# Issuing a kernel's stores from ScalarE's queue in place of SyncE's

## The chip, the core and the metric

The kernel runs on one NeuronCore of a Trainium2 chip. Five engines take their instructions from queues of their own, in order: TensorE (PE; its weight loads are listed as PEld), VectorE (DVE), ScalarE (ACT), GpSimd (POOL) and SyncE (SP). SP computes nothing; in this kernel it issues every transfer (DMA) between the chip's memory and the on-chip buffers. The metric is the device time of one execution in microseconds (us), the median of several runs.

## The reference

Two independent layers are computed over 2048 positions and 576 channels, and their outputs stand side by side in the result (columns 0 to 575 and 576 to 1151).

```python
# A: a state-space layer (S4D) as a long convolution
P = exp((A * dt[:, None])[:, :, None] * pos[None, None, :])        # A, C complex, 576 x 128
K = 2.0 * einsum("dn,dnl->dl", C, P).real                          # one filter per channel
y = irfft(rfft(u_t, 2 * L) * rfft(K, 2 * L)[None], 2 * L)[:, :, :L]
a = y.transpose(0, 2, 1) + u * D_skip

# B: linear attention, 32 heads of 18, with a learned feature map
q, k, v = split_heads(x @ wqkv)
pq, pk = q @ w_phi, k @ w_phi                                      # per head
phi_q = concat([softmax(pq), softmax(-pq)]); phi_k = the same of pk
kv, z = phi_k^T v, sum of phi_k over positions
o = (phi_q kv) / (phi_q z + 1e-6)
b = merge_heads(o) @ wo
out = concat([a, b], axis=-1)
```

All inputs and the output are 32-bit floats.

## The kernel before, in words

**Layer B.** The positions are cut into 16 tiles of 128. `key_tile` loads a tile of x, splits it into a rounded part and a remainder (`x9`, kept in memory as `xd` for later: the split x, stored at L546), multiplies it with the folded key and value weights in three passes per weight, takes the two softmaxes (`softmax`: exponentials on ACT, sums on POOL and DVE) and adds up `kv`. `query_tile` loads `xd` again (L552), makes the query features, transposes them (`fT`), multiplies with `kv`, divides, transposes and splits the result (`x9` again), multiplies with `wo` and copies the product to a tile `ot`, which L739 stores to the output.

**Layer A.** The filters' values come from `phases` (integer angles, on POOL), `waves` (absolute value, sine and cosine on ACT, L909 to L917, which need another function table than the exponentials do, so table loads stand between), and `group` (magnitudes by a product with `sel` and an exponential on ACT, L933 and L940; their products with the waves, `cs` and `E`, on DVE and POOL; and a TensorE product `ps<-E,cs`). The convolution is done by a Fourier transform in two stages, whose first and second stages meet in memory: `u_first` transforms the input u and stores 32 pieces of `ud` (L769, one pair for each of 16 steps); `k_first` does it for the filters and stores 16 pieces of `kd` (L983). These are the two first transforms. `product` loads them (`ub`, `kb`) with its factors (`ff`, L1024), multiplies the spectra and stores the way back to `zd` (L1097, 32 pieces); it starts only when all pieces of `ud` have landed. `last` loads `zd` (L1107), does the final stage and stores rows of the output from tiles `yo` (L1122, 32 pieces). Tiles `zi`, `zo`, `ot` are filled from TensorE's results by copies of ACT and DVE, in shares that the order table fixes.

**What sets the order.** `body` first lists about 2900 operations with their engine, then `Plan.run` gives them out in the order of a table in the file, `ORDER` (L277 on). A number in it is an operation, "*" takes its second engine, "/n" gives the buffer and "+n" adds filler products. Each engine gets its own operations in this one order, so a store's place in the table is also its place in the queue that issues it. The framework adds the semaphores: an issue waits for the writers of its tile, and for transfers that it has to follow. The name in quotes in an `op(...)` call ("sp") is used by the list and its costs; the engine that issues is the one whose `dma_start` is called.

Some places of the table matter below. Store 2446 (L1097, `product` 1) stands behind the DVE copy 2444 and ahead of the ACT operations 2301, 2299, 2302 (L916, L916, L917). Stores 1237, 1238, 1317, 1318, 1198 and 1197 (L769) follow ACT's copies of their tiles. Store 2803 (L1122, `last` 1) stands ahead of ACT's copy 2330 and a table load. Stores 2900 and 2901 (L1122, `last` 15) stand between ACT's two copies 1107 and 1109 of `fT`. The last two operations of the table are ACT's copy 853 of `ot` and its store 854.

Of the kernel before, what the change touches and what calls it, by code (L numbers as in the profile page):

```python
# [266 lines left out]
def c_dma(nbytes, run=4096):  # L267
    return nbytes / run * (0.35 + 0.0029 * run)
# [158 lines left out]
def body(tc, nc, i, out, ctx):  # L427
    pl = Plan()
    pe, dve, act, pool, sp = nc.tensor, nc.vector, nc.scalar, nc.gpsimd, nc.sync
# [14 lines left out]
    B, op = pl.buf, pl.op  # L444
# [236 lines left out]
    def query_tile(t):  # L681
        pl.at("query", t)
        ps = gemm_halves(load_again(t), wqo, (have_q[0:3], have_q[2:5]), 0)
        pl.step("q1")
        e = softmax([(ps[c], slice(16 * c, 16 * c + 16), lambda c=c: ps[c].t.rearrange("p (h f) -> p h f", f=DH)) for c in range(2)], True)
        pl.step("q3")
        fT = []
        rows = lambda j: 18 * GRP[j // 2]

        def turn(j0, n):  # L690
            tp, m, f4 = B("ps", [126, 4, 128]), rows(j0), B("fT", [126, 4, 128])
            fT.append(f4)

            def f():
                for j in range(j0, j0 + n):
                    g, sign = divmod(j, 2)
                    pe.transpose(tp.t[0:m, j - j0, :], e.t[:, sign, 7 * g:7 * g + GRP[g], :].rearrange("p h f -> p (h f)"), ident.t)  # L697
            op("pe", 110 * n, f, r=[e, ident], w=[tp], with_=[f4], busy=0.5)
            copy("any", lambda: f4.t[0:m, 0:n, :], lambda: tp.t[0:m, 0:n], [tp], [f4], 128 * n)
        for j0, n in ((0, 4), (4, 4), (8, 2)):  # L700
            turn(j0, n)
        pl.step("q4")
        o = B("o", [128, H, DH])

        def divide(g0, g1, h0, n):
            pn, den = B("ps", [128, 21, 19]), B("small", [128, 21])

            def f():
                for g in range(g0, g1):
                    hs, m = slice(7 * g, 7 * g + GRP[g]), rows(2 * g)  # L710
                    for sign in range(2):
                        j = 2 * g + sign
                        mm(pn.t[:, hs.start - h0:hs.stop - h0], fT[j // 4].t[0:m, j % 4, :], kvb.t[0:m, sign, 0:GRP[g], g, :], sign == 0, sign == 1)
            op("pe", 448 * (g1 - g0), f, r=[*fT[g0 // 2:(2 * g1 - 1) // 4 + 1], kvb], w=[pn], busy=0.4)
            op("dve", 80 + 6.7 * n, lambda: dve.reciprocal(den.t[:, :n], pn.t[:, :n, 18]), r=[pn], w=[den])
            tt("dve", lambda: o.t[:, h0:h0 + n], lambda: pn.t[:, :n, 0:18], lambda: den.t[:, :n, None].to_broadcast([128, n, DH]),
               ALU.mult, [pn, den], [o], 18 * n)
        divide(0, 3, 0, 21)
        divide(3, 5, 21, 11)
        pl.step("q5")  # L720
        tp, tq = B("ps", [128, 4, 128]), B("ps", [128, 128])
        of = lambda c: o.t.rearrange("p h f -> p (h f)")[:, c:c + 128]

        def f():
            for k in range(4):
                pe.transpose(tp.t[:, k], of(128 * k), ident.t)  # L726
            pe.transpose(tq.t, of(448), ident.t)
        op("pe", 550, f, r=[o, ident], w=[tp, tq], busy=0.5)
        o9 = B("x9", [128, 9, 128], F32R)
        copy("act", lambda: o9.t[:, 0:4], lambda: tp.t, [tp], [o9], 512)  # L730
        tt("dve", lambda: o9.t[:, 5:9], lambda: tp.t, lambda: o9.t[:, 0:4].bitcast(F32), ALU.subtract, [tp, o9], [o9], 512)
        copy("act", lambda: o9.t[64:128, 4], lambda: tq.t[64:128], [tq], [o9], 260)
        tt("dve", lambda: o9.t[0:64, 4], lambda: tq.t[64:128], lambda: o9.t[64:128, 4].bitcast(F32), ALU.subtract, [tq, o9], [o9], 245)
        pl.step("q6")
        po = gemm_halves(o9, wqo, (have_o[0:2], have_o[1:3]), D)
        ot = B("ot", [128, D])
        for c, cs in enumerate(halves):
            copy("any", lambda c=c, cs=cs: ot.t[:, cs], lambda c=c: po[c].t, [po[c]], [ot], 288)
        op("sp", c_dma(128 * 2304, 2304), lambda: sp.dma_start(out[t * 128:t * 128 + 128, 576:1152], ot.t), r=[ot])  # L739

    for t in range(NT):
        query_tile(t)
# [9 lines left out]
    def u_first(k):  # L752
        us, uq, o = B("ub", [128, 2, HD]), B("kb", [128, 2, HD]), B("zi", [128, 4, HD])
        op("sp", c_dma(128 * 2304), lambda: sp.dma_start(us.t.rearrange("p a b -> p (a b)"), i["u"][:, D * k:D * k + D]), w=[us])
        for z, alu in enumerate((ALU.add, ALU.subtract)):
            tt(FLEX, lambda z=z: uq.t[:, z], lambda: us.t[:, 0], lambda: us.t[:, 1], alu, [us], [uq], HD)
        ps = [B("ps", [128, HD]) for _ in range(4)]
        pl.step("u1")

        def f():  # L760
            for z in range(2):
                for m in range(4):
                    rows = slice(32 * m, 32 * m + 32)
                    mm(ps[m].t[64 * z:64 * z + 64], w1.t[rows, 512 + 64 * z:][:, 0:64], uq.t[rows, z])
        op("pe", 520, f, r=[w1, uq], w=ps, with_=[o], mode=(32, 64))
        for m in range(4):
            copy("any", lambda m=m: o.t[:, m], lambda m=m: ps[m].t, [ps[m]], [o], HD)
        for z in range(2):
            op("sp", c_dma(64 * 4608), lambda z=z: sp.dma_start(  # L769
                ud.t[:, 32 * z + 2 * k:32 * z + 2 * k + 2].rearrange("p b d -> p (b d)"), o.t[64 * z:64 * z + 64].rearrange("p m d -> p (m d)")), r=[o], w=[ud])  # L770

    for k in range(16):
# [196 lines left out]
    def k_first(qt, ks):  # L969
        def one(j):  # L970
            o, ps = B("zi", [128, 8, 4, DQ]), [B("ps", [128, 8, DQ]) for _ in range(4)]

            def f():
                for s in range(2):
                    for m in range(4):
                        b0, rows = 8 * (j % 2), slice(32 * m, 32 * m + 32)
                        mm(ps[m].t.rearrange("p b d -> p (b d)"), w1.t[rows, 256 * (j // 2) + 128 * s:][:, 0:128],
                           ks[j // 2].t[rows, s, b0:b0 + 8, :].rearrange("p b d -> p (b d)"), s == 0, s == 1)
            op("pe", 970, f, r=[w1, ks[j // 2]], w=ps, with_=[o], mode=(32, 128))
            for m in range(4):  # L980
                copy("any", lambda m=m: o.t[:, :, m], lambda m=m: ps[m].t, [ps[m]], [o], HD)
            c0, d = qt % 2 * 4 * DQ, kd[qt // 2]
            op("sp", 1.3 * c_dma(128 * 4608, 576), lambda: sp.dma_start(  # L983
                d.t.rearrange("q (r b) d -> (q r) b d", r=2)[:, 8 * j:8 * j + 8, c0:c0 + 4 * DQ],
                o.t.rearrange("p b f d -> p b (f d)")), r=[o], w=[d])
        for j in range(4):
            one(j)
# [8 lines left out]
    par = [None] * NB  # L996
# [21 lines left out]
    def product(p, half):  # L1018
# [75 lines left out]
            copy("any", lambda c=c, j=j, par=par: zo[par].t[:, j], lambda c=c: pz[c].t, [pz[c]], [zo[par]], HD)  # L1094

        for par in range(2):
            op("sp", c_dma(128 * 2304, 1152), lambda par=par: sp.dma_start(four(zd[half], par), zo[par].t), r=[zo[par]], w=[zd[half]])  # L1097

    for half in range(2):
        for p in range(8):  # L1100
# [3 lines left out]
    def last(i0, half):  # L1104
        pl.at("last", 8 * half + i0 // 2)
        yo, zi = B("yo", [128, 2, HD]), B("zi", [128, 2, 2, HD])
        op("sp", c_dma(128 * 4608, 2304), lambda: sp.dma_start(  # L1107
            zi.t, zd[half].t.rearrange("q (r z b) d -> (q r) z b d", r=2, z=2)[:, :, i0:i0 + 2]), r=[zd[half]], w=[zi])
        ps = [B("ps", [128, HD]) for _ in range(2)]
        pl.step("l1")  # L1110

        def f():
            for z in range(2):
                for n in range(2):
                    mm(ps[z].t[64 * n:64 * n + 64], w3.t[:, 64 * z:64 * z + 64], zi.t[:, z, n], True, True, True)
        op("pe", 970, f, r=[zi, w3], w=ps, with_=[yo], mode=(128, 64))
        copy("any", lambda: yo.t[:, 1], lambda: ps[1].t, [ps[1]], [yo], HD)
        for z, alu in enumerate((ALU.add, ALU.subtract)):
            tt("dve", lambda z=z: yo.t[:, z], lambda: ps[0].t, lambda: yo.t[:, 1], alu, [ps[0], yo], [yo], HD)
        for n in range(2):  # L1120
            st = out.ap[0][0]
            op("sp", c_dma(64 * 2304, 1152), lambda n=n: sp.dma_start(bass.AP(  # L1122
                tensor=out.tensor, offset=out.offset + (i0 + n) * st + HD * half, ap=[[32 * st, 64], [(31 - 2 * (i0 + n)) * st, 2], [1, HD]]),
                yo.t[64 * n:64 * n + 64]), r=[yo])

# [25 lines left out]
```

## Time and profile before

| | |
|---|---|
| median of 3 runs | 540.35 us (539.47 to 544.67) |
| profiled execution | 542.0 us, of which the span from first to last instruction 540.2 us |
| PE, DVE, ACT, POOL busy | 519.9, 449.5, 413.8, 331.0 us |
| moved by DMA | 116.41 MB, mean 215 GB/s, all the kernel's own on one queue (q1) |

How to read it: a row of the timeline gives start and length in us, engine, line, operation, tile written <- tiles read, shape and count, and in brackets the idle time before it with what ended it. In the chain of waits a row is start, length and what. SPq and ACTq are the sequencers, which issue and wait and are not counted as busy. In a row of waits stand the total, the number of times and the longest. In a row of one source line come the count and the shortest, median and longest duration in ns, then the first and the last start. In the rows by windows the columns are the stretch, its length, and PE, PEld, DVE, ACT and POOL busy with their counts, then granted clock, share of the DMA engines and GB/s. Lines such as L447 (a product) and L452 (a copy) are helpers that many callers share, so a row is known by its tiles. Matmuls are pipelined, and their ends are modelled.

### The profile page before, as it was taken

Reading aid. Unit: us, or ns where it says so; the run is one execution under the profiler, and the core shown is the slowest. Engines: PE = TensorE matmul, PEld = TensorE weight load, DVE = VectorE, ACT = ScalarE, POOL = GpSimd, SP = SyncE. Lnnn points to the kernel's source line nnn. Section 1 sums busy time; section 2 is a strip of 40 time slices with the busy share of each in tenths; the row PEclk is TensorE's granted clock in tenths of the full one; section 3 lists DMA queues with packets and bytes.
Section 4 is the critical chain, followed back from the end, with each engine's and each line's share of the span. In section 5 each row is a group of like instructions: output and inputs, shape, how many; then the busy total and the mean of one; then the engine's idle time right before and its main releaser. Section 6 shows DMA issues by size and latency. Waiting matters only on the chain.

```text
span 540.2 us, 19689 instructions
## 1 busy us (share of the span) xinstructions
PE 519.9 (96%) x8186; PEld 437.3 (81%) x8186; DVE 449.5 (83%) x994; ACT 413.8 (77%) x730; POOL 331.0 (61%) x375
## 2 busy tenths in 40 slices
PE   6899999999999988999999999999999999999996
PEld 5799998999988767798887767866788887767985
DVE  3799988999999986998988989997986769878463
ACT  2699998999869977989899689799687454564442
POOL 0376798988987975975675579678454354340400
PEclk8999999999999998999999999998999999999999
DMA  8697975923317695573487956696567777997786
GB/s 227 191 358 232 350 229 202 292 80 97 119 45 234 155 324 160 139 234 109 140 225 263 303 158 199 196 277 232 176 194 233 237 216 221 289 340 241 263 265 177
DMA packets 77495, 116.41 MB, mean 215 GB/s; under 512 B 9186, under 2 KB 54370, under 8 KB 77406
## 3 DMA queue, kind: packets, MB, share of 16 engines
q1 hardware_dynamic: 77406, 115.16, 67.9%
q8 instruction: 64, 1.05, 0.8%
q14 instruction: 25, 0.20, 0.1%
HBM read 65.87 MB, written 49.26 MB: 213 GB/s over the span
## 4 chain that ended last, share of the span: by engine, by line
PE 76%; ACT 10%; DVE 6%; DMA 3%; issue 3%; POOL 1%; SPq 0%; DVEq 0%; POOLq 0%; ACTq 0%
PE ps L447 71%; PE ps L697 3%; ACT ps L933 1%; PE ps L726 1%; DMA e<-in_wkT_dram 1%; ACT zi L452 1%; ACT cs L916 1%; ACT cs L917 1%; DMA ff<-in_ff_dram 1%; ACT e L592 1%; DVE cs L944 1%; DMA dram<-zi 1%; ACT cs L909 1%; DVE E L466 1%; DVE wl L514 1%
## 5 line engine op out<-in xcount | busy, mean ns | idle before, releaser
L447 PE MATMUL ps<-wh,x 128*128 128x288 f32 (+2 forms) x1008 | 241.3, 319 | 1.9 <-ACT wh L513 1.4
L447 PEld LDWEIGHTS ps<-wh,x 128*128 128x128 f32 x1008 | 174.3, 189 | 12.8 <-ACT wh L513 1.7
L447 PE MATMUL ps<-wl,x 128*128 128x288 f32 (+2 forms) x560 | 175.9, 315 | 0.4 <-DVE wl L514 0.4
L447 PEld LDWEIGHTS ps<-wl,x 128*128 128x128 f32 x560 | 106.1, 189 | 1.7 <-DVE wl L514 0.7
L899 POOL TENSOR_TENSOR cs<-cs,pi 128x64 int32<-128x64 int32 (+4 forms) x90 | 91.5, 1017 | 6.1
L462 POOL TENSOR_TENSOR E<-v,cs 128x512 f32<-128x512 f32 x30 | 38.5, 1303 | 32.7 <-ACT v L940 31.3
L595 POOL TENSOR_TENSOR o<-e 128x576 f32<-128x576 f32 x32 | 43.1, 1346 | 18.9 <-ACT e L592 16.3
L466 DVE TENSOR_TENSOR ac<-us,ps 128x576 f32<-128x576 f32 x64 | 45.2, 744 | 6.6 <-PE ps L447 5.8
L462 POOL TENSOR_TENSOR e<-e,small 128x576 f32<-128x576 f32 x30 | 36.2, 1208 | 19.6 <-DVE small L462 13.7
L944 DVE TENSOR_TENSOR cs<-ps,cs 128x1024 f32<-128x1024 f32 x36 | 43.7, 1215 | 4.8 <-ACT ps L933 4.7
L447 PEld LDWEIGHTS ps<-E,cs 128*32 128x32 f32 x2304 | 34.6, 110 | 14.3 <-issue 10.3
L447 PEld LDWEIGHTS ps<-kvb,fT 126*128 126x128 f32 (+1 forms) x320 | 39.7, 192 | 7.7 <-issue 1.8
L462 POOL TENSOR_TENSOR e<-small,e 128x576 f32<-128x576 f32 x29 | 34.0, 1172 | 19.4 <-DVE small L462 7.9
L933 ACT ACTIVATE ps<-ps 128x512 f32<-128x512 f32 x72 | 41.6, 588 | 4.4 <-PE ps L447 3.8
L447 PE MATMUL ps<-E,cs 128*32 128x64 f32 x2304 | 40.7, 221 | 4.1 <-issue 3.5
L592 ACT ACTIVATE e<-e 128x1152 f32<-128x1152 f32 x32 | 37.3, 1167 | 8.7 <-POOL e L462 8.7
L447 PE MATMUL ps<-kvb,fT 126*128 126x133 f32 (+1 forms) x320 | 42.9, 284 | 0.6 <-DVE ac L466 0.6
L447 PE MATMUL ps<-sel,mg 128*128 128x512 f32 x108 | 41.5, 443 | 1.4 <-DVE cs L944 0.6
L452 ACT ACTIVATE zi<-ps 128x288 f32<-128x288 f32 x95 | 33.6, 413 | 9.7 <-PE ps L447 9.3
L917 ACT ACTIVATE cs<-cs,hp 128x1024 f32<-128x1024 f32 x36 | 40.6, 1141 | 0.0
L909 ACT ACTIVATE cs<-cs 128x2048 f32<-128x2048 int32 x18 | 34.4, 1913 | 5.8 <-POOL cs L899 5.6
L916 ACT ACTIVATE cs<-cs 128x1024 f32<-128x1024 int32 x36 | 36.7, 1051 | 0.2
(145 smaller groups left out, 1047.4 us busy)
## 6 DMA issues: line engine op xcount, KB each, us to landing
xd<-x SPq DMA_DIRECT2D x16, 576.0 KB
dram<-zi SPq DMA_DIRECT2D x32, 288.0 KB
dram<-zi SPq DMA_DIRECT2D x16, 576.0 KB
x<-xd SPq DMA_DIRECT2D x16, 576.0 KB
kb<-dram SPq DMA_DIRECT2D x32, 288.0 KB
ub<-dram SPq DMA_DIRECT2D x32, 288.0 KB
dram<-zo SPq DMA_DIRECT2D x32, 288.0 KB
zi<-dram SPq DMA_DIRECT2D x16, 576.0 KB
```

The source lines that it names most:

```text
L447: pe.matmul(o, l, r, start=start, stop=stop, skip_group_check=skip)
L452: op(("act", "dve"), (c_act(n), c_dve(n)), lambda e: act.activation(dst(), src(), AF.Copy) if e == "act" else dve.tensor_copy(dst(), src() ...
L462: op(eng, [c_dve(n[0]) if e == "dve" else c_pool(n[1]) for e in eng], lambda e: (dve if e == "dve" else pool).tensor_tensor(dst(), a(), b( ...
L466: op(eng, c_dve(n) if eng == "dve" else c_pool(n), lambda: e.tensor_tensor(dst(), a(), b(), op=alu), r=r, w=w, with_=with_, lock=eng == "p ...
L592: op("act", c_act(1152) + 40, lambda: act.activation(e.t, e.t, AF.Exp), r=[e], w=[e], table="exp")
L595: op("pool", c_pool(517), lambda: pool.tensor_tensor(pair.t, e.t[:, :, :, 0:9], e.t[:, :, :, 9:18], op=ALU.add), r=[e], w=[pair], lock=True)
L899: op("pool", c_add(4 * n * W), lambda n=n, j=j: pool.tensor_tensor(x()[:, :, :, n:2 * n], x()[:, :, :, 0:n], pi.t[:, j:j + 2, gs].bitcast( ...
L909: op(("act", "dve"), (c_act(n) + 45, c_dve(n)), lambda e: act.activation(cs.t[:, 0], x(), AF.Abs) if e == "act" else dve.scalar_tensor_ten ...
L916: op("act", c_act(64 * W) + 150, lambda at=at: act.activation(at(1), at(1).bitcast(I32), AF.Sin, scale=TURN), r=[cs], w=[sine], with_=[cs] ...
L917: op("act", c_act(64 * W) + 225, lambda at=at: act.activation(at(0), at(0), AF.Sin, scale=-TURN, bias=hp.t), r=[cs, hp, sine], w=[both], w ...
L933: op("act", c_act(512) + 12, lambda: act.activation(ps.t, ps.t, AF.Exp), r=[ps], w=[ps], table="exp")
L944: op("dve", c_dve(64 * W), lambda: dve.tensor_tensor(F(), both(M.t), F(), op=ALU.mult), r=[M, ready], w=[long], with_=[cs])
```

## The change

At five places `sp.dma_start` becomes `act.dma_start`: 16 + 32 + 16 + 32 + 32 = 128 stores are issued from ACT's queue. The 16 stores of the split x (L546), a few other stores (L655, L670, L807) and all loads stay with SP. The order table, the buffers and the listed engine "sp" are the same.

```diff
@@ query_tile
-        op("sp", c_dma(128 * 2304, 2304), lambda: sp.dma_start(out[t * 128:t * 128 + 128, 576:1152], ot.t), r=[ot])
+        op("sp", c_dma(128 * 2304, 2304), lambda: act.dma_start(out[t * 128:t * 128 + 128, 576:1152], ot.t), r=[ot])
@@ u_first
-            op("sp", c_dma(64 * 4608), lambda z=z: sp.dma_start(
+            op("sp", c_dma(64 * 4608), lambda z=z: act.dma_start(
@@ k_first
-            op("sp", 1.3 * c_dma(128 * 4608, 576), lambda: sp.dma_start(
+            op("sp", 1.3 * c_dma(128 * 4608, 576), lambda: act.dma_start(
@@ product
-            op("sp", c_dma(128 * 2304, 1152), lambda par=par: sp.dma_start(four(zd[half], par), zo[par].t), r=[zo[par]], w=[zd[half]])
+            op("sp", c_dma(128 * 2304, 1152), lambda par=par: act.dma_start(four(zd[half], par), zo[par].t), r=[zo[par]], w=[zd[half]])
@@ last
-            op("sp", c_dma(64 * 2304, 1152), lambda n=n: sp.dma_start(bass.AP(
+            op("sp", c_dma(64 * 2304, 1152), lambda n=n: act.dma_start(bass.AP(
```

## The prediction

> **What bounds the kernel now.** I read the page first: busy shares, slices, the chain of waits.
>
> ```profile
> span 540.2 us, 19689 instructions
> PE 519.9 (96%) x8186; PEld 437.3 (81%) x8186; DVE 449.5 (83%) x994; ACT 413.8 (77%) x730; POOL 331.0 (61%) x375
> ...
> ACT  2699998999869977989899689799687454564442
> ...
> PE 76%; ACT 10%; DVE 6%; DMA 3%; issue 3%; POOL 1%; SPq 0%; DVEq 0%; POOLq 0%; ACTq 0%
> ```
>
> TensorE is busy for 519.9 of 540.2 us, and 76% of the chain that ended last lies on it. ScalarE (ACT) has 540.2 - 413.8 = 126.4 us idle, unevenly spread: its digits are mostly 8 and 9 for two thirds of the span and 4 to 6 later. The queue of SyncE (SP), where all transfers are issued now, has 0% of the chain. So the change relieves an engine that limits nothing and loads one that holds a tenth of the chain.
>
> Next I asked where TensorE is idle (windows of 30 us) and for what it waits.
>
> ```profile
> 0.00:30.00 30.00, 23.90 (x160) 20.98 (x161) 17.08 (x42) 15.74 (x33) 8.37 (x24) 0.89 0.80 224
> 180.00:210.00 30.00, 25.38 (x673) 19.48 (x673) 22.94 (x49) 25.89 (x48) 23.84 (x29) 0.94 0.75 238
> 510.00:540.00 30.00, 26.06 (x208) 21.84 (x206) 12.64 (x31) 11.10 (x26) 2.80 (x3) 1.00 0.77 236
> ```
> ```profile
> PE ps L447 <- issue: 5.7, 4, 1.8
> PE ps L447 <- DMA e<-in_wkT_dram: 2.6, 1, 2.6
> PE ps L447 <- DMA ff<-in_ff_dram: 0.4, 1, 0.4
> ```
>
> The first number behind the stretch's length is TensorE's busy time. Of its 540.2 - 519.9 = 20.3 idle us, 6.1 lie in the first 30 us, 4.6 between 180 and 210, 3.9 in the last stretch: 5.7 in all the rest. Its waits for a transfer are 2.6 us at the start, before the first store, and 0.4 us in the middle. There is little that an earlier load could give back.
>
> **What an issue costs and how much ACT can hide.** The change moves 16 + 32 + 16 + 32 + 32 = 128 issues, priced by the rows of the five lines (shortest / median / longest, ns):
>
> ```profile
> L739 SPq DMA_DIRECT2D out_dram<-ot x16: 337/354/1266, 252.6 to 536.5; - x16
> L769 SPq DMA_DIRECT2D dram<-zi x32: 445/599/1851, 39.3 to 276.7; - x32
> L983 SPq DMA_DIRECT2D dram<-zi x16: 359/374/1107, 159.1 to 436.6; - x16
> L1097 SPq DMA_DIRECT2D dram<-zo x32: 359/421/1402, 298.8 to 502.2; - x32
> L1122 SPq DMA_DIRECT2D out_dram<-yo x32: 595/604/1324, 410.1 to 534.8; - x32
> ```
>
> By medians: 16 x 0.354 + 32 x 0.599 + 16 x 0.374 + 32 x 0.421 + 32 x 0.604 = 63.6 us leave SP and come to ACT. No issue by ACT is in this trace; SP's are the nearest rows, and I take their shortest where the queue is not crowded. Not all of it delays ACT:
>
> ```profile
> L452 ACTq EVENT_SEMAPHORE  x1: 17/17/17, 181.8 to 181.8; - x1
> 180.97 2.17 ACT L917 ACTIVATE cs<-cs,hp 128x1024 f32<-128x1024 f32 x2
> ```
>
> ACT's sequencer handled a semaphore at 181.8, while its engine was busy until 183.14. So a store whose tile is ready can be issued underneath the ACTIVATE in front of it. It costs time in three cases: it waits for DVE's half of the tile and holds ACT; the copy just in front of it is itself the last writer, so nothing covers it; or it comes ahead of a table load. Most stores fall between ready and covered, since the order table puts them some operations behind their writers. [...]
>
> **The four places that cost most, and the rest.**
>
> (a) Store 2446 of `product` 1 (L1097), ahead of ACT's four sine passes.
>
> ```profile
> 376.85 2.01 ACT L916 ACTIVATE cs<-cs 128x1024 f32<-128x1024 int32 x2
> 383.83 0.58 ACT L933 ACTIVATE ps<-ps 128x512 f32<-128x512 f32 x1 [1.60 <-PE ps L447]
> 380.69 0.43 DVE L452 COPY zo<-ps 128x288 f32<-128x288 f32 x1
> 381.15 0.36 SPq L1097 DMA_DIRECT2D dram<-zo  x1
> 385.88 0.68 DVE L950 SCALAR_TENSOR_TENSOR E<-ps,cs 128x512 f32<-128x512 f32 x1
> 389.62 1.10 PE L447 MATMUL ps<-E,cs 128*32 128x64 f32 x64
> ```
>
> DVE finishes this tile at 380.69 + 0.43 = 381.12, and SP waited for that with nothing lost. On ACT the same wait stands in front of the pass at 376.85, which now starts after 381.15 + 0.36 = 381.51: 4.7 us late. The 1.60 us idle before 383.83 take up some: the exponential (L933) is 3.1 late, ending 387.5. DVE's L950, at 385.88 before, waits for it and is 1.6 late, and DVE has little idle time from there to the last factor of TensorE's products at 389.62, which I put 1.2 later. **+1.2 us**; bounds 0 (other slack) and 4.7 (none).
>
> (b) The last six stores of the input's first transform (L769), which the second stage of the products needs.
>
> ```profile
> 269.32 1.32 ACT L452 ACTIVATE zi<-ps 128x288 f32<-128x288 f32 x4 [1.36 <-PE ps L447]
> 276.18 1.74 SPq L769 DMA_DIRECT2D dram<-zi  x2
> 276.67 4.43 DMA dram<-zi
> 287.03 1.81 PE L447 MATMUL ps<-ub,ff 64*32 64x288 f32 x32 [0.35 <-DMA ff<-in_ff_dram]
> ```
>
> Each stands behind ACT's own copies of its tile. Four follow the last of these directly and cost their 0.45 us each; two hide mostly under a copy of another tile, which I put at 0.15 each: 2.1 us by the time of the last, which lands that much later, and the chain goes from its landing over the loads to the TensorE products at 287.03, which already waited. Against that, the last two issues took 1.74 us on the crowded SP queue where the shortest would be 2 x 0.445: 0.85 back. **+1.3**; bounds -0.9 and 2.1.
>
> (c) Store 2803 of `last` 1 (L1122).
>
> ```profile
> 408.95 0.27 ACT L452 ACTIVATE ks<-ps 128x128 f32<-128x128 f32 x1
> 409.66 0.45 DVE L466 TENSOR_TENSOR yo<-ps,yo 128x288 f32<-128x288 f32 x1
> 410.14 1.37 SPq L1122 DMA_DIRECT2D out_dram<-yo  x2
> 411.87 2.53 POOL L462 TENSOR_TENSOR E<-v,cs 128x512 f32<-128x512 f32 x2 [12.74 <-ACT v L940]
> 415.22 0.99 PE L447 MATMUL ps<-E,cs 128*32 128x64 f32 x56
> ```
>
> ACT's copy at 408.95 now follows the store, at 410.14 + 0.6 = 410.74: 1.8 late. Behind it ACT has no gap up to the exponential that POOL's E waits for, so E ends at 414.40 + 1.8 = 416.2 against TensorE's need at 415.22. **+1.0**; bounds 0 and 1.8.
>
> (d) Stores 2900 and 2901, ahead of ACT's second transposed copy of the last query tile.
>
> ```profile
> 520.40 1.08 ACT L452 ACTIVATE fT<-ps 126x512 f32<-126x512 f32 x2 [2.16 <-PE ps L697]
> 520.98 1.90 SPq L1122 DMA_DIRECT2D out_dram<-yo  x3
> 522.01 1.01 DVE L466 TENSOR_TENSOR x<-ps,x 128x512 fp32r<-128x512 f32 x2 [0.69 <-ACT x L455]
> 523.61 0.38 PE L447 MATMUL ps<-wh,x 128*128 128x288 f32 x1
> ```
>
> Two issues of 0.6 from 520.98 push the second of these copies from 520.9 to 522.2, 1.3 late. The split that ends at 523.02 becomes 524.3, past 523.61: 0.7 by this path, up to 1.3 by the products that read the copy. **+1.0**; bounds 0 and 1.3.
>
> (e) The other 117 stores. The chain stands on ACT for 10%, so at most about a tenth of 63.6 us, 6.4, meets it uncovered; at least 0. Two of them (L769) come ahead of a table load and would push it by 2 x 0.45. **+1.5**, nearer to 0, as ACT has idle time behind most.
>
> (f) What SP gains: its loads stop waiting behind stores. TensorE's waits for transfers in the middle are 0.4 us, and the transfers in the chain from 276.67 on hang on the last store, counted in (b). **0**; at best the 4.6 idle us of 180 to 210.
>
> Sum: 1.2 + 1.3 + 1.0 + 1.0 + 1.5 = 6.0 us. The profiled execution took 542.0 us, 1.8 beyond its span; it would take 548.0. The median before, 540.35, is 1.65 lower, so I forecast 546.4 (548.0 - 1.65). The bounds add to between -5.5 and +16.3; taken together 541.5 to 553 is the forecast's own range.
>
> **Rivals.** *ACT's idle time swallows it* (540 to 543): against the four places stands that TensorE runs in order and waits for what ACT makes; for it, that all four delays are under 5 us in 540 and that ACT's gaps elsewhere take in many of that size, as the 1.60 us in (a). Only the tail of (d) remains, about 1 us.
>
> *Faster, through SP* (531 to 537). SP stands still in front of stores while loads wait behind:
>
> ```profile
> SPq L983 <- DVE zi L452: 37.4, 8, 15.0
> SPq L489 <- DMA ks<-in_mag_dram: 1.1, 1, 1.1
> ```
>
> If loads that now start up to 15.0 us sooner ended half or more of TensorE's roughly 10 idle us between start and tail, it would gain 5 to 9, less what ACT loses. It decides once an earlier load removes more than ACT's 6 us. Against it: the waits above name almost no load. [...]
>
> *ACT's queue is choked* (552 to 562). The second row above shows an issue held by the landing of an unrelated transfer. An ACT that must wait for such landings, at 1.1 us for each of some ten stores between 40 and 300 us where its digits are 8 and 9, and pays crowded issues (up to 1851 ns in the L769 row) with no cover, loses another 6 to 15 us.
>
> **Chances.** Forecast 0.48, swallowed 0.28, choked 0.14, faster 0.10. This kernel's measurement tells about 1% from no change, 5.4 us. Slower by more: the choked case and some two thirds of the forecast's, 0.45; faster by more: nearly all of the rival's, 0.09; within: 0.46. A range of 537 to 555 leaves out most of the faster rival below and half of the choked case above, with the forecast's extremes: 2 in 10.
>
> **What would show it.** In the changed profile: 128 issues on ACT, each 0.34 to 0.6 us; ACT busy unchanged, but its first sine pass near 377 starting after DVE's `zo` copy, 4 to 5 us late; TensorE's idle time up by about 6 us, near 389, 415, 287 and 522 (all moved on by what went before); waits of TensorE or DVE that name ACT, not DMA. I am wrong if ACT's issues are much shorter or lie wholly under ACTIVATEs, if SP's earlier loads remove TensorE's idle time of 180 to 210, or if ACT waits for landings at many stores.

## The result, and the profile after

The changed kernel takes 568.98 us (median of 565.02 to 570.50), the kernel before 542.14 us in the runs beside it. The ratio is 1.0468, with a 95% interval of 1.0427 to 1.0509: 25.4 us slower (23.1 to 27.6). (The plain difference of the two medians, 26.8, is the +27 of some expectations below.) The forecast was 546.4 and its range ended at 555. The profiled execution took 565.0 us, 23 more than the profiled one before.

The page of the changed kernel: span, busy times, ScalarE's slices, and the chain of waits.

```profile
span 563.2 us, 19653 instructions
PE 528.7 (94%) x8186; PEld 436.0 (77%) x8186; DVE 452.3 (80%) x994; ACT 414.1 (74%) x730; POOL 329.4 (58%) x375
...
ACT  4797988998779796899798688896785454454442
...
PE 36%; ACT 23%; DVE 16%; DMA 7%; issue 6%; POOL 6%; ACTq 4%; SPq 0%; POOLq 0%; DVEq 0%
```

ACT's own work is the same (414.1 us against 413.8), and so are the matmuls (8186). TensorE's idle time went from 20.3 to 563.2 - 528.7 = 34.5 us. The 8.8 us by which its busy time also grew are not read further, because the ends of matmuls are modelled. The chain has changed in kind: TensorE held 76% of it and holds 36% now, while ACT and DVE together went from 16 to 39%.

The rows by windows, first for two stretches of the kernel before, then for the same of the changed one (TensorE's busy time is the number behind the stretch's length):

```profile
60.00:90.00 30.00, 30.00 (x536) 28.26 (x535) 27.94 (x61) 28.06 (x41) 25.07 (x31) 1.00 0.78 273
420.00:450.00 30.00, 30.00 (x347) 25.74 (x347) 20.95 (x56) 14.89 (x33) 12.03 (x11) 1.00 0.75 227
```
```profile
60.00:90.00 30.00, 27.96 (x494) 26.25 (x482) 26.71 (x58) 26.49 (x38) 22.71 (x28) 1.00 0.77 247
420.00:450.00 30.00, 27.92 (x378) 22.36 (x376) 19.02 (x47) 15.22 (x34) 10.20 (x8) 1.00 0.66 203
```

Stretches without any idle time of TensorE now have some 2 us of it. The loss is spread over the whole kernel. The granted clock isn't the cause: over the whole execution it is 0.990, and 0.987 before (it differs in two stretches only, 0 to 30 us with 1.00 against 0.89 and 210 to 240 us with 0.94 against 1.00). When the start of each matmul is set against that of the same matmul before, TensorE is 3.2 us ahead at 30 us (before the first stores, so this lead is not the change's), and behind by 2.7 at 100, 8.2 at 290, 14.6 at 405 and 23.0 at 534 (times of the kernel before). It is a staircase of about twenty steps of 0.5 to 2.7 us. (Each kernel has one profiled execution. Read in this way, it drifts by some 2 us where nothing was changed: the kernel with `yo` alone, whose first moved store is issued at 411 us, is 0.9 behind at 30, 2.6 at 370 and 0.8 at 405. So such figures are good for single steps and less so for sums.)

The issues themselves cost what the forecast said (rows by source line: shortest / median / longest, ns):

```profile
L739 ACTq DMA_DIRECT2D out_dram<-ot x16: 338/357/2190, 258.3 to 560.1; - x16
L769 ACTq DMA_DIRECT2D dram<-zi x32: 452/453/1962, 34.7 to 285.9; - x32
L983 ACTq DMA_DIRECT2D dram<-zi x16: 361/372/1105, 161.8 to 454.4; - x16
L1097 ACTq DMA_DIRECT2D dram<-zo x32: 361/367/596, 307.4 to 523.9; - x32
L1122 ACTq DMA_DIRECT2D out_dram<-yo x32: 602/618/1462, 424.7 to 557.8; - x32
```

Who waits for ACT, before and after (total, times, longest; us):

```profile
POOL E L462 <- ACT v L940: 31.3, 7, 12.7
PEld ps L447 <- ACT zi L452: 4.8, 13, 0.7
DVE cs L944 <- ACT ps L933: 4.7, 5, 2.4
```
```profile
POOL E L462 <- ACT v L940: 42.1, 8, 14.4
DVE cs L944 <- ACT ps L933: 13.6, 13, 3.0
PEld ps L447 <- ACT zi L452: 10.0, 15, 2.7
PE ps L447 <- ACT zi L452: 3.9, 4, 2.2
PE ps L447 <- DMA kb<-dram: 0.4, 1, 0.4
```

What grew are the waits of DVE, GpSimd and TensorE for ACT. TensorE's waits for a transfer in the middle are still 0.4 us, and 0.9 us for its weight loads.

**ACT's lost time, counted.** For each store, in the order of ACT's queue, I took from the trace two times: the *wait*, from the end of the last ACT operation ahead of it to the start of its issue, and the *open issue*, the part of the issue that lies after that end. For the 128 stores the open issue is 41.1 us and the wait 15.9 us, 57.0 together. Of the wait, 11.4 us are for DVE's part of the tile, at 17 stores. Only 34 stores are issued wholly underneath work ahead of them (to within 0.03 us). (The expectations below speak of 64.0 us held. That first count took the operation in front by time and not by the queue's order, and so counted some issues as open that ran underneath work ahead.)

### The profile page after: what moved, and what is told of

Read it like the earlier page. It is cut to its first block, busy times and chain, and to the rows that moved or that the text cites. A ratio compares the mean times of both kernels' runs of the same rounds, so it can differ in the third digit from the quotient of the medians.

```text
span 563.2 us, 19653 instructions
## 1 busy us (share of the span) xinstructions
PE 528.7 (94%) x8186; PEld 436.0 (77%) x8186; DVE 452.3 (80%) x994; ACT 414.1 (74%) x730; POOL 329.4 (58%) x375
## 4 chain that ended last, share of the span: by engine, by line
PE 36%; ACT 23%; DVE 16%; DMA 7%; issue 6%; POOL 6%; ACTq 4%; SPq 0%; POOLq 0%; DVEq 0%
PE ps L447 34%; ACT zi L452 3%; ACT cs L917 3%; POOL cs L899 3%; ACT cs L916 2%; DMA ub<-in_u_dram 2%; DVE cs L944 2%; ACT ps L933 2%; PE ps L697 2%; ACT cs L909 2%; ACTq L1122 2%; ACTq L769 1%; DVE yo L466 1%; ACT L933 1%; ACT e L592 1%
## 5 line engine op out<-in xcount | busy, mean ns | idle before, releaser
L447 PE MATMUL ps<-wh,x 128*128 128x288 f32 (+2 forms) x1008 | 241.1, 319 | 1.8 <-ACT zi L452 0.9
L447 PEld LDWEIGHTS ps<-wh,x 128*128 128x128 f32 x1008 | 174.0, 189 | 13.6 <-issue 3.0
L447 PE MATMUL ps<-wl,x 128*128 128x288 f32 (+2 forms) x560 | 175.5, 314 | 0.4 <-DVE wl L514 0.4
L447 PEld LDWEIGHTS ps<-wl,x 128*128 128x128 f32 x560 | 105.8, 189 | 1.6 <-DVE wl L514 0.7
L944 DVE TENSOR_TENSOR cs<-ps,cs 128x1024 f32<-128x1024 f32 x36 | 43.8, 1217 | 13.7 <-ACT ps L933 13.6
L462 POOL TENSOR_TENSOR e<-e,small 128x576 f32<-128x576 f32 x30 | 35.8, 1195 | 23.1 <-DVE small L462 15.7
L447 PE MATMUL ps<-sel,mg 128*128 128x512 f32 x108 | 43.3, 452 | 6.5 <-ACT v L940 1.9
L462 POOL TENSOR_TENSOR e<-small,e 128x576 f32<-128x576 f32 x29 | 34.0, 1173 | 23.1 <-DVE small L462 11.7
L447 PEld LDWEIGHTS ps<-kvb,fT 126*128 126x128 f32 (+1 forms) x320 | 40.0, 193 | 9.3 <-issue 1.9
L447 PEld LDWEIGHTS ps<-E,cs 128*32 128x32 f32 x2304 | 34.7, 110 | 14.0 <-issue 8.9
L447 PE MATMUL ps<-kvb,fT 126*128 126x133 f32 (+1 forms) x320 | 43.7, 286 | 1.9 <-ACT fT L452 1.2
L592 ACT ACTIVATE e<-e 128x1152 f32<-128x1152 f32 x32 | 37.3, 1167 | 10.3 <-POOL e L462 10.2
L447 PE MATMUL ps<-E,cs 128*32 128x64 f32 x2304 | 40.8, 221 | 3.5 <-issue 2.6
L452 ACT ACTIVATE zi<-ps 128x288 f32<-128x288 f32 x95 | 33.7, 416 | 13.0 <-PE ps L447 10.3
```

The costliest lines, as they stand in the source:

```text
L447: pe.matmul(o, l, r, start=start, stop=stop, skip_group_check=skip)
L452: op(("act", "dve"), (c_act(n), c_dve(n)), lambda e: act.activation(dst(), src(), AF.Copy) if e == "act" else dve.tensor_copy(dst(), src() ...
L462: op(eng, [c_dve(n[0]) if e == "dve" else c_pool(n[1]) for e in eng], lambda e: (dve if e == "dve" else pool).tensor_tensor(dst(), a(), b( ...
L592: op("act", c_act(1152) + 40, lambda: act.activation(e.t, e.t, AF.Exp), r=[e], w=[e], table="exp")
L944: op("dve", c_dve(64 * W), lambda: dve.tensor_tensor(F(), both(M.t), F(), op=ALU.mult), r=[M, ready], w=[long], with_=[cs])
```

## The experiments

Two theories stood against each other. *Held time*: ACT runs in order (in the changed kernel its 730 operations start in the order of its queue), so what it loses in issuing and waiting passes on to TensorE, wherever it lies. *Transfers*: stores in ACT's queue land later or hold up loads, and the cost comes with what is loaded again. A third reading is the forecast's own: *only the four places* cost.

### One family of stores at a time

Each kernel changes `sp` to `act` at one line (the last at two):

```diff
-            op("sp", c_dma(64 * 4608), lambda z=z: sp.dma_start(
+            op("sp", c_dma(64 * 4608), lambda z=z: act.dma_start(
```

> Only the 32 stores of ud (L769) are issued from ACT; all others stay with SP. In the trace of the changed kernel these 32 hold ACT for 15.0 of the 64.0 us that all stores hold it (time from the end of ACT's work in front to the end of the issue, as far as nothing of ACT runs above it), and the whole change cost about 25 us. Theory 'held time': ACT has no slack to TensorE almost anywhere, so a family costs its share of the held time: 25 x 15.0 / 64.0 = +5.9 us over the kernel before (4 to 8). Rival 'landings': the cost comes from transfers that are loaded again (ud, kd, zd) and land later, and from loads held back; then ud, with a quarter of the stores and the longest issues among these three, costs a third or more of the 25, +8 to +12. Rival of the forecast 'only the four places': +1.3 (the last six stores).

> Only the 32 stores of zd (L1097) are issued from ACT. They hold ACT for 16.2 of 64.0 us in the changed kernel. Theory 'held time': 25 x 16.2 / 64.0 = +6.3 us (4 to 9). Rival 'landings': zd is loaded again by the last stage, so +8 to +12. 'Only the four places': +1.2 (store 2446).

> Only the 32 stores of the tiles yo (L1122) are issued from ACT. They hold ACT for 21.4 of 64.0 us, about 4 of them after TensorE's last products. They go to the output, and nothing in the kernel loads what they write. Theory 'held time': 25 x (21.4 - 4) / 64.0 = +6.8 us, up to 2 more through the tail (5 to 9). Rival 'landings': nobody waits for them, so -1 to +2. 'Only the four places': +2.0 (stores 2803, 2900, 2901).

> Only the 16 stores of kd (L983) and the 16 of ot (L739) are issued from ACT. They hold ACT for 6.0 + 5.4 = 11.4 of 64.0 us. Theory 'held time': 25 x 11.4 / 64.0 = +4.5 us (2 to 6). Rival 'landings': kd alone is loaded again, with 16 stores, +2 to +5, so this run tells the two apart least. 'Only the four places': 0.

Measured (a ratio of r is given as (r - 1) x 542 us): `ud` 1.0115 (1.0054 to 1.0177), +6.2 us; `zd` 1.0125 (1.0043 to 1.0206), +6.8; `yo` 1.0114 (1.0072 to 1.0155), +6.2; `kd` and `ot` 1.0087 (1.0044 to 1.0131), +4.7. The sum is 23.9 of 25.4 us.

All four stand close to the figures of held time. For `ud` and `zd` the intervals reach into the range of the rival (+8 to +12). The one that counts most is `yo`: nothing loads what these stores write, and most of them lie where ACT is half idle (14.89 of 30 us in the row above), yet they cost as much as the others. So this family's loss doesn't come from transfers that are loaded again, and idle time on ACT isn't slack. The loss also lies where the stores lie: with `ud` alone TensorE loses 8.1 us between 30 and 290 us and nothing behind it.

The forecast's place (a) can be seen by itself in the kernel with `zd` alone (timeline of ACT):

```profile
378.35 1.90 ACT L909 ACTIVATE cs<-cs 128x2048 f32<-128x2048 int32 x1
381.44 0.37 ACTq L1097 DMA_DIRECT2D dram<-zo  x1
381.86 2.01 ACT L916 ACTIVATE cs<-cs 128x1024 f32<-128x1024 int32 x2 [1.60 <-DVE us L452]
```

ACT is free at 378.35 + 1.90 = 380.25 and stands until DVE's copy is done. The sine pass behind the store starts at 381.86.

### Copies in place of the issues

Here SP issues all stores again, and ACT gets a small copy at each of the 128 places, either of the stored tile (it waits for the tile's writers) or of a constant. In `held`, `d` is a part of a scratch tile of the same shape. (The kernels below have a few lines more or less than the one before, so the same helper has another number in their rows: L470 and L446 are the product L447, L475 the copy L452, L467 the new copy. To make room for the scratch tile, two small tiles of the filters' parameters are merged and three DVE operations stand later; what that alone costs wasn't measured.)

```diff
+    def both(dma, n, src):
+        dma()
+        for s in src():
+            held(n, s)
...
+        act.activation(d, s, AF.Copy)
-    lambda par=par: sp.dma_start(four(zd[half], par), zo[par].t)
+    lambda par=par: both(lambda: sp.dma_start(four(zd[half], par), zo[par].t), 192, lambda: [zo[par].t[:, :, 0:96]])
```

> No store is moved: SP issues all, as before the change. Instead, at each of the 128 places ACT makes a small copy (192 elements per partition; for yo two of 144) of a part of the tile that is stored, written by both engines that fill it, into a scratch tile that nobody reads. So ACT waits for the same writers as the moved store would, and is then held for about the time of an issue (0.3 to 0.35 us by the 0.27 us of a 128x128 copy; about 50 us in all), with no transfer in its queue. (To make room for the scratch tile, three small DVE operations of the filters' parameters stand a few places later.) Theory 'held time': ACT's lost time alone makes the loss, so +18 to +32 us, as the whole change cost +27. Rival 'transfers' (landings, crowded issues, late loads): no transfer has moved, so 0 to +4.

> As the run with copies of the stored tile, but the small copies at the 128 places read a constant tile (w1) that is always ready: ACT is held for about 50 us in all and waits for nobody. Theory 'held time', with the issue as its larger part (47.9 of 64.0 us held were issue not covered by an ACTIVATE, the rest waits): 25 x 50 / 64 = +19 us (12 to 25), less than the run that also waits by 3 to 9. Rival 'only the waits hurt' (the order of the queue, not the time of the issue): 0 to +5. Rival 'transfers': 0 to +4.

Measured: with waits 1.0345 (1.0316 to 1.0375), +18.7 us; without 1.0178 (1.0129 to 1.0227), +9.7 us. The rows of the kernel with waits (copies by form, then ACT's waits for DVE at them):

```profile
L467 ACT ACTIVATE scr<-yo x64: 306/323/384, 422.5 to 554.6; 128x144 bf16<-128x144 f32 x64
...
ACT scr L467 <- DVE zo L475: 4.3, 5, 1.8
ACT scr L467 <- DVE yo L489: 4.0, 6, 1.1
ACT scr L467 <- DVE zi L475: 2.0, 2, 1.7
```

So ACT's time alone, with no transfer in its queue, makes some three quarters of the loss. I had put the larger part on the issue; that fell. ACT is busy for 453.6 us with the copies of a constant, 39.8 more than before, and this costs 9.7 us: 0.24 us for each us of plain work. With the copies that wait ACT is busy for 457.6 us, 43.8 more, and it waits 4.3 + 4.0 + 2.0 = 10.3 us. At 0.24 the work makes 10.7 of the 18.7 us; the other 8.0 come with 10.3 us of waiting, 0.78 for each. A us that ACT waits for DVE costs about three times as much as a us in which it works. The intervals of the two runs leave 0.18 to 0.31 for the first rate and some 0.5 to 1.1 for the second, so that the second is the larger is shown, and by how much is not.

Two families were done in the same manner, to be set beside the stores themselves.

> All stores on SP; small ACT copies (192 elements per partition) of the stored tile only at the 32 places of the stores of ud (L769). With those 32 stores on ACT the loss was 6.0 us in the medians (8.1 of TensorE's time between 30 and 290 us). 32 copies of 0.27 us are 8.7 us of ACT's time, against 11.8 us of issue that no ACTIVATE covered there, and no copy waits for a landing (2.8 us there). Theory 'held time alone': in proportion to 8.7 + 1.7 (own copy) of 15.3 us held, +4 (3 to 5). If landings, crowded issues and the transfers themselves made most of that loss: 0 to +2.

> All stores on SP; two small ACT copies (144 elements each) of the stored tile at each of the 32 places of the stores of yo (L1122), which wait for DVE as the store does. With those 32 stores on ACT the loss was 5.5 us in the medians. 64 copies of 0.27 us are 17 us, against 14.5 us of uncovered issue there, and the same waits. Theory 'held time': +4 to +7. Rival 'transfers': 0 to +1.

Measured: `ud` 1.0061 (1.0020 to 1.0102), +3.3 us against 6.2 with the stores; `yo` 1.0118 (1.0079 to 1.0157), +6.4 against 6.2. For `yo` the copies give the whole loss, with somewhat more of ACT's time (17.4 us busy, against 12.9 us of open issue). This is the forecast's place (c) there, on ACT:

```profile
408.60 0.41 ACT L475 ACTIVATE yo<-ps 128x288 f32<-128x288 f32 x1 [1.02 <-PE ps L470]
410.09 0.68 ACT L467 ACTIVATE scr<-yo 128x144 bf16<-128x144 f32 x2 [1.09 <-DVE yo L489]
410.68 0.26 ACT L475 ACTIVATE ks<-ps 128x128 f32<-128x128 f32 x1
```

The copy of `ks` started at 408.95 before and starts at 410.68 now, with not one store moved, and TensorE loses 1.6 us from 405 to 417 us. For `ud` the copies give about half, but the two intervals touch.

### The stores later in the order

The order table is changed so that each store on ACT stands behind two (or one) further ACT operations. Store 2446 as an example (operations of other engines between are left out):

```diff
-2446 2301 2299 560/7/18
+2301 2299 2446 560/7/18
```

> All 128 stores on ACT as in the change, but in the order table each stands behind two further ACT operations (122 of them two, 3 one, 3 none), so that its tile is mostly ready and the issue can run underneath the ACTIVATE in front of it. Theory 'held time': both the waits and most of the uncovered issues go, the held time falls from 64 to some 10 to 20 us, and the loss from 27 to +3 to +9 us. Rival 'transfers' (the stores in ACT's queue, crowded issues, landings that come later): the same transfers in the same queue, and all of them later, so +22 to +32. Between the two, +10 to +20, if ACT cannot issue underneath an ACTIVATE.

> As the run with two operations, but each store stands behind one further ACT operation only (125 of 128). Its own copy is then done, DVE's half not always, and the operation in front covers 0.3 to 1.1 us. Theory 'held time': most of the uncovered issues go and some of the waits stay, +5 to +13 us, above the run with two operations by 2 to 6. Rival 'transfers': +22 to +32.

Measured: two operations later 1.0366 (1.0313 to 1.0420), +19.9 us; one later 1.0427 (1.0351 to 1.0503), +23.2 us. Both expectations of held time failed: the loss hardly fell. But the trace divides the run with two operations. At 405 us TensorE is 3.6 us behind, where the change itself was 14.6 behind; from there to 534 us it loses 11.2 us, and 4 more in the tail. Two runs ask what happens in the second part: the same order with all stores on SP, and only the early stores on ACT.

```diff
+    def dma_start(self, *a):
+        (self.act if self.now in EARLY else self.sp).dma_start(*a)
```

> All stores on SP as before, but in the order table of the run in which each stands two ACT operations later. That run lost 11.2 us of TensorE's time from 405 us on and 4 more in the tail. If that loss comes from the later place (where ACT's operations are far apart, the stores land later, tiles come free later and zd is loaded later), it stays without ACT's queue: +8 to +15 us. If it comes from ACT still being held by issues, it goes: 0 to +3.

> The 67 stores that SP issued before 405 us of the kernel before are on ACT, each two ACT operations later (65 two, 1 one, 1 none); the 61 later ones stay with SP in their old places. With all stores on ACT two operations later, TensorE was only 3.6 us behind at that place, while the change itself was 14.6 behind. Theory 'held time': stores that are covered by an ACTIVATE cost little, +2 to +5 us. Rival 'transfers': the same 67 transfers in the same queue as in the change, +11 to +16. If taking 67 stores from SP is worth anything, it would show here as 0 or below.

Measured: that order on SP 1.0175 (1.0116 to 1.0235), +9.5 us; the 67 early stores 1.0078 (1.0048 to 1.0108), +4.2 us. So about half of the 19.9 us (9.5, with an interval of 6.3 to 12.7) belongs to the later place itself, without ACT's queue. The waits of TensorE for transfers show a part of it (before they were 0.5 us for `ub` and none for `kb`):

```profile
PEld ps L446 <- DMA ub<-dram: 1.9, 2, 1.2
PE ps L446 <- DMA kb<-dram: 1.8, 3, 0.8
PE ps L446 <- DMA ub<-dram: 1.8, 2, 1.1
```

Where stores stand behind longer ACT operations they can be hidden. ACT of the early run:

```profile
252.92 1.90 ACT L919 ACTIVATE cs<-cs 128x2048 f32<-128x2048 int32 x1
253.47 0.36 ACTq L226 DMA_DIRECT2D dram<-zi  x1
```

The issue (L226 is the helper that issues in this kernel) lies wholly underneath the pass. Of the 67 early stores 56 are so (to within 0.04 us), and the open issue is 4.0 us in all. The kernel is still 4.2 us slower than before. How much of that is their later place isn't measured; whatever SP gains by 67 stores less doesn't outweigh it.

### Twelve stores that were held or long

In the changed kernel some issues wait for an unrelated landing, as at 53.71 (ACT idle for 2.45 us until `mg` has landed), and some last over 1 us (the longest, at L739, 2.19):

```profile
53.71 0.46 ACTq L769 DMA_DIRECT2D dram<-zi  x1
54.22 0.28 ACT L840 ACTIVATE ax<-ax 128x96 f32<-128x96 f32 x1 [2.45 <-DMA mg<-gd]
```

The last open question was whether the part of the loss that the copies don't show lies there. One kernel issues all stores but such twelve from ACT (the diff), the other these twelve alone.

```diff
+HELD = {1208, 1218, 1227, 1268, 1328, 1277, 971, 2831, 2845, 2381, 2399, 2851}
+        (self.act if self.now not in HELD else self.sp).dma_start(*a)
```

> All stores on ACT in the old order but for twelve, which SP issues: 1208, 1218, 1227, 1268, 1277, 1328 (L769), 971 (L739), 2381, 2399 (L983), 2831, 2845, 2851 (L1122). In the changed kernel or in the runs of single families these waited for a transfer's landing or had issues far longer than the shortest of their line; together that is some 11 us of ACT's time beyond a plain issue. The loss with all on ACT was +27, with copies that wait in their place +19. Theory 'ACT is held, and the last 8 us by landings and crowded issues': +16 to +21. Rival 'proportional' (the twelve cost no more than others, or their waits pass to other stores): 27 x 116 / 128 = +24.5 (23 to 27).

> Only these twelve stores are on ACT, in the old order; the other 116 stay with SP. Theory 'landings and crowded issues': they meet the same landings, so +4 to +9. Rival 'proportional': 27 x 12 / 128 = +2.5 (1 to 4).

Measured: without the twelve 1.0373 (1.0328 to 1.0419), +20.3 us; only the twelve 1.0014 (0.9976 to 1.0052), +0.8 us. The two answers contradict the theory as it was put. Taking the twelve away gives back some 5 us (2 to 9 by the two intervals, where their share would be 2.4); alone they cost nothing that can be told from zero. The trace suggests why: a wait isn't a property of these stores. With only the twelve on ACT, store 1208 is issued underneath the work ahead of it and waits for no landing:

```profile
52.47 0.49 ACT L459 ACTIVATE v<-ps 128x396 f32<-128x396 f32 x1
52.61 0.51 ACTq L222 DMA_DIRECT2D dram<-zi  x1
52.86 1.15 ACT L924 ACTIVATE cs<-cs,hp 128x1024 f32<-128x1024 f32 x1
```

And without the twelve, another store (1297) stands in front of the same landing, for 2.03 us of ACT's idle time:

```profile
58.81 0.45 ACTq L222 DMA_DIRECT2D dram<-zi  x1
59.31 0.63 ACT L462 ACTIVATE sel<-v 128x512 fp32r<-128x512 f32 x1 [2.03 <-DMA mg<-gd]
```

Which store meets a landing depends on what else delays ACT in that run. So the loss has to be held against the lost time of each run's own trace.

### All runs against ACT's lost time

The estimate takes 0.24 for each us of open issue and 0.78 for each us of wait, the two rates from the copies alone. (There the rate of a wait comes from waits for DVE only; here all waits are counted.)

| stores on ACT | open issue, us | wait, us | estimate | measured (95%) |
|---|---|---|---|---|
| `ud` | 8.7 | 3.5 | 4.8 | 6.2 (2.9 to 9.6) |
| `zd` | 9.0 | 4.8 | 5.9 | 6.8 (2.3 to 11.2) |
| `yo` | 12.9 | 4.4 | 6.5 | 6.2 (3.9 to 8.4) |
| `kd`, `ot` | 9.8 | 2.3 | 4.1 | 4.7 (2.4 to 7.1) |
| early 67, two later | 4.0 | 1.7 | 2.3 | 4.2 (2.6 to 5.9) |
| all, two later | 21.3 | 4.8 | 8.9 | 19.9 - 9.5 = 10.4 (6.1 to 14.7) |
| only the twelve | 3.2 | 0.5 | 1.2 | 0.8 (-1.3 to 2.8) |
| without the twelve | 34.0 | 10.8 | 16.6 | 20.3 (17.8 to 22.8) |
| all (the change) | 41.1 | 15.9 | 22.3 | 25.4 (23.1 to 27.6) |

Two rates found without any store on ACT give most of the loss of every row. They stay 1 to 4 us short for the largest ones, and that rest stays open. Slower transfers are not it: from the start of the issue to the last count of the transfer's semaphore the stores of `zi` tiles take 4.5 us (median) before and in the changed kernel, those of `zo` 3.4 and 3.6, of `ot` 3.3 and 3.5, of `yo` 3.3 and 2.8. Stores that are issued later, and so land later, are possible; no run separates them. In the row of the 67 early stores the cost of their later place isn't taken off. The run with one operation later isn't in the table for the same reason: it has 27.8 us of open issue and 6.1 us of wait, an estimate of 11.4 of its 23.2 us, and what its order costs on SP wasn't measured. No kernel tried is faster than the one before.

## Why the prediction was wrong

**The failing step is (e), "the other 117 stores".** It took the share of ACT in the chain, 10%, as an upper bound for what passes from ACT to TensorE, gave 6.4 us at most, and chose 1.5 "as ACT has idle time behind most". From 3.2 us ahead before the first store TensorE ends 23.0 behind; with the four places taken off as read below, some 16 to 20 us are left for these stores (118 by count, as the four places hold ten). Three things were wrong in it. It took most stores for ready and covered; in the trace 34 of the 128 are covered. The chain is the path as it stood: a share of 10% says how much of that path lies on ACT, not how far ACT's other work is from becoming the path. With 0.4 us more in front of many operations the path moved onto them: ACT's share went to 23%, DVE's to 16%. And the wait was counted only where a row had been looked at, 4.7 us in (a) and 1.8 in (c), while the trace has 11.4 us for DVE at 17 stores and 15.9 in all, at the rate that costs most.

**(a)** was right in its mechanism, and too small. In the changed kernel the sine pass of 376.85 starts at 393.60 and the product of 389.62 at 403.71:

```profile
392.72 0.43 DVE L452 COPY zo<-ps 128x288 f32<-128x288 f32 x1
393.18 0.37 ACTq L1097 DMA_DIRECT2D dram<-zo  x1
393.60 2.01 ACT L916 ACTIVATE cs<-cs 128x1024 f32<-128x1024 int32 x2 [3.20 <-DVE us L452]
403.71 1.10 PE L447 MATMUL ps<-E,cs 128*32 128x64 f32 x64
```

The product is 14.1 us late where TensorE was 11.8 late at 370 and still at 377: +2.3 instead of +1.2. In the kernel with `zd` alone the step from 377 us to this product is 2.2 us, and with the copies that wait 2.1. The wait of the store ahead of it in the same stretch is in that too; the prediction had not named it.

**(b)** came near in its size, and by another way. From 269 us, ahead of these six stores, to the products of `ub` TensorE loses 1.5 us, in the changed kernel (7.3 to 8.8 late) as in the one with `ud` alone (5.8 to 7.3); right behind them 0.6 comes back. The forecast was 1.3. But these products don't wait for anything now, neither for the last store's landing nor for a load. What TensorE waited for were ACT's copies behind the stores (rows of the changed kernel):

```profile
279.07 0.49 PE L447 MATMUL ps<-sel,mg 128*128 128x512 f32 x1 [0.22 <-ACT ot L452]
288.17 1.13 PE L447 MATMUL ps<-kvb,fT 126*128 126x133 f32 x8 [0.37 <-ACT fT L452]
295.83 1.20 PE L447 MATMUL ps<-ub,ff 64*32 64x288 f32 x32
```

**(c)** and **(d)** were right in their mechanism, (c) somewhat too small. The product now has to wait for GpSimd's E, and the second transposed copy is what TensorE waits for:

```profile
428.18 2.51 POOL L462 TENSOR_TENSOR E<-v,cs 128x512 f32<-128x512 f32 x2 [14.38 <-ACT v L940]
430.74 0.99 PE L447 MATMUL ps<-E,cs 128*32 128x64 f32 x56 [0.15 <-POOL E L462]
545.18 1.59 PE L447 MATMUL ps<-kvb,fT 126*128 126x133 f32 x12 [0.57 <-ACT fT L452]
```

The product of 415.22 starts 15.0 late, the part of it that waits for E stands in the row above, and by 417 us TensorE is 16.3 late: 1.7 more than at 405 (forecast 1.0, bound 1.8), and 1.8 in the kernel with `yo` alone. From 520 to 534 us it loses 0.9 (forecast 1.0).

**(f)** was right as far as the runs show: nothing comes back from SP that could be seen. Its waits passed from the tiles' writers to landings, for instance of `dram<-zo` at L1107, 24.6 us, and no engine that computes gained.

**The price of an issue** was right (0.34 to 0.62 us, 67.6 us in all against 63.6 by medians). That a ready store can be issued underneath the ACTIVATE in front was right too: 34 of the 128 are. ACT's sequencer goes further ahead than that one, see below.

**The rivals.** "ACT's idle time swallows it" is wrong by the run with `yo`. "Faster, through SP" is wrong by the result; the run with the early stores, where ACT loses little, isn't faster either. "ACT's queue is choked" had the right side, and its price, 552 to 562, was nearest; but it put the cost on landings and crowded issues, and these are the smaller part: copies without any transfer already give 18.7 us.

**What would show it**: that TensorE's waits name ACT and not DMA was right. That its idle time would lie near 389, 415, 287 and 522 was wrong: it lies in nearly every stretch.

## What to carry to other kernels

In a kernel like this one, in which TensorE is nearly always busy (96% here) and two or three engines feed it in a fixed order, price work that is moved to a feeding engine with a share of its whole time that isn't covered, at every place (here 0.24 for each us worked), and not with that engine's share in the chain or its idle time. Price waits apart and higher (here 0.78): list for each moved instruction which writer it waits for and whether that writer is another engine, because here an issue from the queue of an engine that computes stopped all that stood behind it (none of the ACT operations behind the 128 stores starts before the issue ahead of it has ended). SP does nothing else here, and its waits cost nothing: 0% of the chain before.

## What the runs showed of the hardware

ACT's sequencer runs ahead of its engine by up to four operations in the changed kernel. Store 1328 stands behind all four operations below in the queue's order, and its issue starts before the last three of them do:

```profile
198.44 0.59 ACT L933 ACTIVATE ps<-ps 128x512 f32<-128x512 f32 x1
198.57 1.96 ACTq L769 DMA_DIRECT2D dram<-zi  x1
198.92 0.29 ACT L513 ACTIVATE wh<-ps 128x126 fp32r<-128x126 f32 x1
199.08 0.30 ACT L840 ACTIVATE ax<-ax 128x96 f32<-128x96 f32 x1
199.25 1.02 ACT L529 ACTIVATE wh<-e 128x960 fp32r<-128x960 f32 x1
```

At four of the 128 stores four operations ahead of the issue were still to start; at the one issued at 42.23 us a table load, which starts at 43.77, is among them. What this doesn't change is the order behind an issue: 127 of the stores have an ACT operation behind them, and each of these operations starts 0.03 us or more after the issue has ended. A table load is held in the same way: the operation ahead of the store issued at 65.79 us ended at 65.29, the issue ended at 66.26, and the load behind it starts at 66.29, after 0.99 us of idle time. No run shows a gain from having two engines issue; the smallest loss, +0.8 us with the twelve stores alone, can't be told from zero. The change shows that it costs 25.4 us here when an engine that computes has to issue, the waits of its queue included.
